# Which engine issues the first weight strips: three of four W1 strips move from SyncE to ScalarE

## The chip, the cores and the metric

The kernel runs on one core of a Trainium2 chip. The metric is the device time of one execution in microseconds (us). Before the change it is 163.12 us, the median of 3 runs (163.06 to 163.18).

## What is computed

x is 2048 rows of 512 bf16 numbers. Two branches and a gate are computed from it and mixed:

```python
qkv = x @ wqkv                    # 32 heads of 16
# a: each position attends to the 8 positions s, s-2, ..., s-14 of its head, then @ wo
h = layernorm(x, axis=-1)         # over the 512 columns, no weights
u = gelu(einsum("bsd,sf->bdf", h, w1) + b1)    # w1 is 2048 x 1792: it mixes the rows
b = transpose(einsum("bdf,fs->bds", u, w2) + b2)
g = sigmoid((x * gate_w).sum(-1, keepdims=True))
out = g * a + (1 - g) * b
```

## The kernel before

x is cut into 16 tiles X[:, t, :] of 128 rows (128 KB each). The first four of them are treated apart, and everything that this change concerns is in how they start.

**The lead.** For tiles 0 to 3, VectorE (DVE) takes the row statistics (`stat`, line 622; `aggr`, line 626), ScalarE (ACT) makes 1/sqrt(var) of them as Exp(-0.5 Ln(var)) (`rstd`, lines 629 and 630), and DVE writes the normalized tile LX (`apply`, line 633). TensorE (PE) then multiplies each with the first 512 columns of the same 128 rows of W1, a "strip" LW[:, t, :] of 128 KB, four matmuls to a tile (`f_lead`, line 617). PE also transposes the four x tiles (`f_tx`, line 585), the biases b1 and b2 (`f_tb`, lines 601 and 602) and spreads the gate's weights over the partitions by a matmul with ones ("gwbc", line 642). PE's order is written out by hand by a chain of order edges: five warm-up matmuls, tx0, tx1, the bias transposes, tx2, gwbc, lead0, tx3, lead1, lead2, lead3. ACT copies the transposed tiles from PSUM (`ext`), DVE the last one.

**After the lead.** PE computes the projections k, q, v (line 712, 192 matmuls) from the transposed x and WQKV; the first of them, "pjk", takes the first half of Wk ("wk01") alone. ACT copies them out. Then come W1 for all 16 tiles (line 608), W2 (line 937) and the output product with wo (line 946). DVE meanwhile multiplies q by shifted k, and the products are summed over a head's columns by 16 small matmuls for each half of the rows (line 803, "sum0" and "sum1"), which stand between the W1 matmuls in PE's order. Statistics of x tiles 4 to 15 (line 775) and the gate's sums (line 756) are DVE's too; those of tile 4 stand ahead of its first q-k product.

**What sets the order.** A small planner in the kernel (`_Sched`) simulates all operations with a duration for each and writes one fixed program for each engine. An operation waits for its producers by semaphores. Loads go through `load` (line 494; the DMA itself is at line 500, a transposing one at line 499). Those on SyncE's queue ("sp") are chained in the order in which the code names them: x0, x1, x2, strip 0, x3, strips 1, 2, 3, wk01, wk23, wq, x4 (tiles 4 and 5), then the transposing load xt1, x6, xt2, x8, xt3, x12, wv, W1 and so on. ACT issues three small loads in front of its work: b1, b2 and the gate's weights gw, which wait for POOL's zeroing of their tile (line 478). Its first table load stands behind these, because `emit_engine` puts a table load in front of the first activation that needs one:

```python
        def emit_engine(eng_name, e):
            table = None
            for op in sch.order[eng_name]:
                if eng_name == "act" and not op.is_dma:
                    want = TABLE.get(op.name, table or LOGEXP)
                    if want != table:
                        e.preload_act_table_set(want)
                        table = want
```

Of the kernel before, what the change touches and what calls it, by code (L numbers as in the profile page):

```python
# [13 lines left out]
D = 512  # L14
# [16 lines left out]
GL = 4  # L31
# [259 lines left out]
class _Mem:  # L291
# [17 lines left out]
    def view(self, name, dtype, dims, extra=0, p0=0, np_=128):  # L309
        base = self.arena[:].bitcast(dtype)  # L310
        pst = base.ap[0][0]
        esz = mybir.dt.size(dtype)
        o = self.off[name]
        assert o % esz == 0
        return bass.AP(base.tensor, p0 * pst + o // esz + extra, [[pst, np_]] + [list(d) for d in dims])


def bass_gated_mix__sliding_local_dilated__mixer_token_mlp__prompt_kernel(nc, A_x, A_wqkv, A_wo, B_x, B_w1, B_b1, B_w2, B_b2, gate_w, out, dbg=None):
    with contextlib.ExitStack() as es:
# [37 lines left out]
        def psub(ap_, p0, np_, offs, dims):  # L357
            pst = ap_.ap[0][0]
            return bass.AP(ap_.tensor, ap_.offset + p0 * pst + offs, [[pst, np_]] + [list(d) for d in dims])
# [9 lines left out]
        w1v = B_w1.rearrange("(st p) f -> p st f", p=128)  # L369
# [21 lines left out]
        LW = view("LOG", BF16, [(128 * GL, NLEAD), (1, 128 * GL)])  # L391
# [23 lines left out]
        GW1 = psub(GWZ, 0, 1, 0, [(1, D)])  # L415
# [10 lines left out]
        B1R = view("ROWS", BF16, [(1, 128)], np_=NFT)  # L426
        B2R = view("ROWS", BF16, [(1, 128)], extra=128, np_=NST)
# [30 lines left out]
        def col(v_, i):  # L458
            return bass.AP(v_.tensor, v_.offset + i, [list(v_.ap[0]), [1, 1]])
# [31 lines left out]

        last_ld = [None]

        def load(name, dst, src, nbytes, writes, transpose=False, queue="sp", issue=0.5, order=True, deps=(), reads=()):
            ds = sch.dsem(name)

            def fn(e):
                if transpose:
                    return e.dma_start_transpose(dst, src)
                return e.dma_start(dst, src)  # L500
            op = sch.dma(queue, fn, nbytes, ds, issue=issue, reads=reads, writes=writes, deps=deps,
                         after=([last_ld[0]] if order and last_ld[0] is not None else []), name=name)
            if order:
                last_ld[0] = op
            return op

        def ld_x(t0, n):
            load("x%d" % t0, X[:, t0:t0 + n, :], xv[:, t0:t0 + n, :], n * 128 * D * 2, ["x%d" % t for t in range(t0, t0 + n)])

        def ld_w(name, tn, d0, d1, res):  # L510
            load(name, WQKV[:, d0:d1, tn * D:(tn + 1) * D], wqkv_v[:, d0:d1, tn * D:(tn + 1) * D], (d1 - d0) * 128 * D * 2, [res])

        def ld_xt(sb):
            load("xT%d" % sb, XT[:, :, sb * 512:(sb + 1) * 512], x2d[sb * 512:(sb + 1) * 512, :], int(1.4 * 512 * D * 2), ["xt%d" % sb],
                 transpose=True)
# [1 line left out]
        def ld_wq(name, d0, d1, res):  # L517
            load(name, WQKV[:, d0:d1, 0:D], wqkv_v[:, d0:d1, 0:D], (d1 - d0) * 128 * D * 2, [res], queue="act", order=False)

        def ld_strip(t, n):  # L520
            load("s%d" % t, LW[:, t:t + n, :], w1v[:, t:t + n, 0:128 * GL], n * 32768 * GL, ["lw%d" % t_ for t_ in range(t, t + n)])

        ld_x(0, 1)
        ld_x(1, 1)
        ld_x(2, 1)
        ld_strip(0, 1)
        ld_x(3, 1)
        ld_strip(1, 1)
        ld_strip(2, 1)
        ld_strip(3, 1)  # L530
        ld_w("wk01", 1, 0, 2, "wk")
        ld_w("wk23", 1, 2, 4, "wk2")
        load("gw", GW1, bass.AP(gate_w.tensor, gate_w.offset, [[D, 1], [1, D]]), 1024, ["gwr"], issue=0.4, queue="act", order=False)
        load("b1", B1R, B_b1.rearrange("(t p) -> t p", p=128), 4096, ["b1r"], issue=0.4, queue="act", order=False)
        load("b2", B2R, B_b2.rearrange("(t p) -> t p", p=128), 4096, ["b2r"], issue=0.4, queue="act", order=False)
        ld_w("wq", 0, 0, 4, "wq")
        ld_x(4, 2)
        ld_xt(1)
# [53 lines left out]
        def ext(t, eng, after):  # L592
            bank, o = TXB[t]
            src = sub(psb(bank), o, [(128, 4), (1, 128)])
            dst = sub(XT, t * 128, [(S, 4), (1, 128)])
            if eng == "dve":
                return A("dve", lambda e: e.tensor_copy(out=dst, in_=src), 0.42, reads=["b%d" % bank], writes=["xt0_%d" % t], after=after, name="ext%d" % t, prio=-30)
            return A("act", act(dst, src, AF.Copy), 0.6, reads=["b%d" % bank], writes=["xt0_%d" % t], after=after, name="ext%d" % t, prio=-30)
# [69 lines left out]
        e3 = ext(3, "dve", [ag])  # L668
        l3 = apply(3, [e3])
        e3 = l3  # L670
# [61 lines left out]
        for dl in range(4):  # L732
# [3 lines left out]
          reads=["k%d_1" % dl for dl in range(4)], writes=["khalo"], name="khalo")  # L736
# [18 lines left out]
        for t in range(NST):  # L755
            A("dve", (lambda t_: lambda e: e.tensor_tensor_reduce(out=JUNK[:, t_ % 4, :], in0=X[:, t_, :], in1=GWB, scale=1.0, scalar=0.0, op0=ALU.mult, op1=ALU.add,  # L756
                                                                  accum_out=col(Z, t_)))(t), 0.61, reads=["x%d" % t, "gwb", "s4"], writes=["z%d" % t, "jk%d" % (t % 4)], after=[e3],
              name="z%d" % t, prio=-4)
        A("pool", lambda e: e.memset(ZN, 0.0), 0.15, writes=["zn"], name="zn0")
        A("dve", lambda e: e.tensor_scalar(out=ZN[:, 0:NST], in0=Z, scalar1=ZMAX, scalar2=-1.0, op0=ALU.min, op1=ALU.mult), 0.12,  # L760
          reads=["z%d" % t for t in range(NST)], writes=["zn"], name="zneg", prio=-30)
# [11 lines left out]

        for t in range(NLEAD, NST):
            A("dve", (lambda t_: lambda e: e.bn_stats(out=ST6[:, t_, :], in_=X[:, t_, :]))(t), 0.6,  # L775
              reads=["x%d" % t], writes=["st%d" % t], after=[e3], name="st%d" % t, prio=-4, delay=1.0 if t == 4 else 0.0)
        STS = ["st%d" % t for t in range(NLEAD, NST)]
        A("dve", tt(MS, ST_m0, ST_m1, ALU.add), 0.12, reads=STS, writes=["ms"], name="ln_ms", prio=-20)
        A("dve", tt(MD, ST_m0, ST_m1, ALU.subtract), 0.12, reads=STS, writes=["md"], name="ln_md", prio=-20)
# [4 lines left out]
          reads=["md"], writes=["vv"], name="ln_var", prio=-20)  # L784
# [3 lines left out]
          reads=["ms", "rstd"], writes=["nmr"], name="ln_nmr", prio=-20)  # L788
        for t in range(NLEAD, NST):
            if t >= NST - LNACT:  # L790
                A("act", act(X[:, t, :], X[:, t, :], AF.Identity, scale=col(RSTD2, t), bias=col(NMR, t)), 0.7, after=[ev2[0][t - NST - 1]], reads=["rstd", "nmr"], writes=["x%d" % t],
                  name="ln%d" % t)
            else:
                A("dve", (lambda t_: lambda e: e.tensor_scalar(out=X[:, t_, :], in0=X[:, t_, :], scalar1=col(MS, t_), scalar2=col(RSTD2, t_),
                                                               op0=ALU.subtract, op1=ALU.mult))(t), 0.33,
                  reads=["rstd", "ms", "st%d" % t], writes=["x%d" % t], name="ln%d" % t, prio=-4)
# [14 lines left out]
        for h in range(2):  # L811
# [43 lines left out]
            if h == 0:  # L855
                A("dve", tt(psub(LOG[0], 0, 32, 0, [(UT_, NW), (1, PAD)]), psub(LOG[0], 0, 32, 0, [(UT_, NW), (1, PAD)]), MASK, ALU.add), 0.2,
                  reads=["mask"], writes=["log0"], name="msk")
# [16 lines left out]
            for c in range(4):  # L874
                for dhi in range(4):
                    src = psub(ATT[h], 32 * c, 32, 0, [(1, NW * UT_)])
                    pst = AVW[h].ap[0][0]
                    dst = bass.AP(AVW[h].tensor, AVW[h].offset + dhi * pst + c * NW * UT_, [[4 * pst, 32], [1, NW * UT_]])
                    ds = sch.dsem("av%d_%d_%d" % (h, c, dhi))
                    prev = sch.dma("pool", (lambda d_, s_: lambda e: e.dma_start(d_, s_))(dst, src), 131072, ds, issue=1.0,  # L880
                                   reads=["att%d" % h], writes=["avw%d_%d_%d" % (h, c, dhi)] + al, after=[prev] if prev else [],
                                   name="av%d_%d_%d" % (h, c, dhi))
# [10 lines left out]
        for u in range(8):  # L893
# [5 lines left out]
              reads=["avw%d_%d_%d" % (h, c, dhi) for dhi in range(4)] + vr + ["vpad"], writes=PR[b], name="avm%d" % u)  # L899
# [15 lines left out]
        for ft in range(NFT):  # L915
            bank = ft if ft < GL else bank_()
            s0 = NLEAD if ft < GL else 0
            for a_, b_ in ((s0, 8), (8, NST)):
# [3 lines left out]
              reads=["b%d" % bank, "b1c"], writes=["ut%d" % ft] + (["wq", "wk", "wk2", "wv"] if ft == 0 else []), name="gel%d" % ft)  # L922
# [69 lines left out]
        for hf, (c0, c1) in enumerate(CH):  # L992
# [3 lines left out]
            if hf == 0:  # L996
                A("act", act(OUTS[:, NOUT, c0:c1], ps[:, bank, 0:n_], AF.Identity, scale=col(OMG, L), bias=col(C2, L)), 0.4,
                  reads=["b%d" % bank, "omg", "c2"], writes=["outl%d" % hf], name="ev%d_%d" % (L, c0))
# [5 lines left out]
        LOGEXP = "natural_log_exp_and_others"  # L1004
# [16 lines left out]

        def emit_engine(eng_name, e):
            table = None
            for op in sch.order[eng_name]:
                if eng_name == "act" and not op.is_dma:
                    want = TABLE.get(op.name, table or LOGEXP)
# [3 lines that stand above are left out]
                for d in op.waits:  # L1030
                    if d.is_dma:
                        e.wait_ge(d.dsem.handle, 16 * d.seq)
                    else:
                        e.wait_ge(esem[d.eng], d.seq)
                r = op.fn(e)
                if isinstance(r, list):
                    r = r[-1]
                if op.is_dma:
                    r.then_inc(op.dsem.handle, 16)
                elif op.sig:  # L1040
                    r.then_inc(esem[eng_name], 1)
            if eng_name == "sp":
                for d in ds_out + ds_last:
                    e.wait_ge(d.handle, 16 * d.count)

        emit_engine("sp", nc.sync)
        emit_engine("act", nc.scalar)
        emit_engine("pool", nc.gpsimd)
        emit_engine("dve", nc.vector)
        emit_engine("pe", nc.tensor)  # L1050
# [28 lines left out]
```

## Time and profile before

| | us |
|---|---|
| median of 3 runs | 163.12 (163.06 to 163.18) |
| profiled execution, its own time | 163.36 |
| span in the profile, first to last instruction | 162.1 |
| PE busy | 158.8 (98%) |
| DVE busy | 150.9 (93%) |
| ACT busy | 77.7 (48%) |
| POOL busy | 27.2 (17%) |

TensorE's granted clock is 1.0 throughout. The profile comes from one execution, which lies 0.24 us above the median; 1.26 us of its time lie outside the span.

How to read the views used below. The *chain of waits* follows the end back to the start: at each step to what released the instruction. Its rows are start, length, engine and line. In the *timeline* a row is start, length, engine, line, operation, tiles, count; in brackets stands how long the engine had been idle and what ended that. SPq and ACTq are DMA issues by SyncE and ScalarE, so a row of them is the issue, not the transfer. The *list of DMA issues* in a stretch gives, for the issues that fall in it, the time from issue to landing.

### The profile page before, as it was taken

How to read it: one execution, taken by the hardware profiler on the slowest of the kernel's cores; microseconds unless marked ns; L12 is line 12 of the kernel's file. 1: busy time of each engine (PE TensorE's matmuls, PEld its weight loads, DVE VectorE, ACT ScalarE, POOL GpSimd, SP SyncE). 2: the span in 40 equal slices, each digit the busy share in tenths (PEclk: the TensorE clock that was granted, in tenths of full speed). 3: DMA queues.
4: the chain of work that ended last, by engine and by line, in shares of the span. 5: the costliest groups of instructions: out<-in, count | busy, mean ns of one | idle time of the engine just before them, and what ended most of it. 6: DMA issues, size and time to landing. Idle time of an engine off the chain costs nothing.

```text
span 162.1 us, 2008 instructions
## 1 busy us (share of the span) xinstructions
PE 158.8 (98%) x778; PEld 75.7 (47%) x778; DVE 150.9 (93%) x143; ACT 77.7 (48%) x103; POOL 27.2 (17%) x63
## 2 busy tenths in 40 slices
PE   7999999999999999999999999999999999999994
PEld 3445555555554444444444444444444444444652
DVE  2968999999999999999999999999999999999963
ACT  3817765679999471699511344420111111111153
POOL 4000003000000002020595030007590003020000
DMA  4799989999952998999299999999999921959604
GB/s 132 224 258 209 243 194 328 257 213 212 287 174 82 298 294 193 240 266 216 55 311 363 350 299 306 212 297 289 345 220 204 194 92 50 200 131 194 142 32 162
DMA packets 45287, 35.54 MB, mean 219 GB/s; under 512 B 8029, under 2 KB 42078, under 8 KB 45278
## 3 DMA queue, kind: packets, MB, share of 16 engines
q1 hardware_dynamic: 41376, 22.74, 53.5%
q0 software_dynamic: 3696, 12.59, 35.6%
q8 instruction: 6, 0.10, 0.3%
q10 hardware_dynamic: 206, 0.08, 0.2%
q14 instruction: 3, 0.02, 0.0%
HBM read 19.15 MB, written 2.11 MB: 131 GB/s over the span
## 4 chain that ended last, share of the span: by engine, by line
PE 95%; DMA 2%; SPq 1%; DVE 0%; issue 0%
PE ps L937 30%; PE ps L608 28%; PE ps L712 26%; PE ps L946 9%; DMA arena<-in_B_w_dram 2%; PE ps L617 2%; SPq L500 1%; PE ps L803 1%; DVE arena L955 0%
## 5 line engine op out<-in xcount | busy, mean ns | idle before, releaser
L468 DVE TENSOR_TENSOR arena<-arena 128x4096 bf16<-128x4096 bf16 (+6 forms) x71 | 125.6, 1806 | 1.3
L937 PE MATMUL ps<-arena 128*128 128x512 bf16 (+2 forms) x238 | 50.2, 366 | 0.0
L471 ACT ACTIVATE arena<-ps,arena 128x512 bf16<-128x512 f32 (+1 forms) x29 | 20.9, 728 | 54.3 <-PE ps L946 40.1
L608 PE MATMUL ps<-arena 128*128 128x512 bf16 x208 | 45.4, 379 | 0.0
L712 PE MATMUL ps<-arena 128*128 128x512 bf16 x192 | 41.6, 379 | 0.0
L471 ACT ACTIVATE arena<-ps 128x512 bf16<-128x512 f32 (+3 forms) x38 | 31.7, 843 | 14.4 <-PE ps L712 11.1
L937 PEld LDWEIGHTS ps<-arena 128*128 128x128 bf16 x238 | 23.3, 98 | 25.4
L608 PEld LDWEIGHTS ps<-arena 128*128 128x128 bf16 x208 | 20.2, 98 | 24.9 <-issue 0.8
L712 PEld LDWEIGHTS ps<-arena 128*128 128x128 bf16 x192 | 21.7, 113 | 19.8 <-issue 0.3
L880 POOL DMA_DIRECT2D arena<-arena x32 | 17.1, 664 | 23.1 <-DVE arena L468 14.0
L471 ACT ACTIVATE arena<-arena 128x512 bf16<-128x512 bf16 (+6 forms) x27 | 15.2, 564 | 11.5 <-DVE arena L468 10.4
L946 PE MATMUL ps<-arena 128*128 128x512 bf16 (+2 forms) x68 | 15.6, 366 | 0.0
L831 POOL DMA_DIRECT2D arena<-arena x3 | 3.8, 1270 | 63.4 <-DVE arena L468 63.4
L1028 ACT ACT_TABLE_LOAD x9 | 11.5, 1283 | 2.3 <-POOL arena L479 2.2
L756 DVE CUSTOM_DVE_ANT_0 arena<-arena 128x512 bf16<-128x512 bf16 x16 | 10.1, 683 | 0.0
L901 POOL DMA_DIRECT2D arena<-arena x4 | 4.9, 1226 | 31.1 <-DVE arena L468 31.1
L946 PEld LDWEIGHTS ps<-arena 128*128 128x128 bf16 x68 | 6.6, 98 | 7.2
L775 DVE BATCH_NORM_STATS2 arena<-arena 128x6 f32<-128x512 bf16 x12 | 7.4, 680 | 2.3 <-DMA arena<-in_A_x_dram 2.3
L622 DVE BATCH_NORM_STATS2 arena<-arena 128x6 f32<-128x512 bf16 x4 | 2.7, 678 | 3.0 <-DMA arena<-in_A_x_dram 2.9
L617 PE MATMUL ps<-arena 128*128 128x512 bf16 x16 | 3.8, 378 | 0.2
L955 DVE TENSOR_SCALAR arena<-ps,arena 128x512 bf16<-128x512 f32 (+1 forms) x2 | 1.3, 659 | 2.7 <-PE ps L946 2.6
L567 PE MATMUL ps<-const-bfloat16-1.0 128*128 128x512 bf16 x5 | 2.3, 625 | 0.8 <-PEq L1064 0.8
(39 smaller groups left out, 18.7 us busy)
## 6 DMA issues: line engine op xcount, KB each, us to landing
arena<-in_B_w_dram SPq DMA_DIRECT2D x8, 896.0 KB, 13.5
arena<-arena POOLq DMA_DIRECT2D x6, 1024.0 KB, 9.8
arena<-in_B_w_dram SPq DMA_DIRECT2D x5, 1024.0 KB, 9.5
arena<-arena POOLq DMA_DIRECT2D x32, 128.0 KB, 7.5
arena<-arena POOLq DMA_DIRECT2D x1, 2048.0 KB, 17.9
out_dram<-arena SPq DMA_DIRECT2D x15, 128.0 KB, 1.8
arena<-in_B_w_dram SPq DMA_DIRECT2D x2, 768.0 KB, 13.4
arena<-in_A_wqkv_dram SPq DMA_DIRECT2D x2, 512.0 KB, 5.7
```

What stands on the lines that cost most here:

```text
L468: return lambda e: e.tensor_tensor(out=o_, in0=a_, in1=b_, op=op_)
L471: return lambda e: e.activation(out=o_, in_=i_, func=f_, **kw)
L608: ins = e.matmul(ps[:, bank, :], lhsT=W1S[W1AT[ft // 2]][:, st, 128 * (ft % 2):128 * (ft % 2) + 128], rhs=(LX if st < NLEAD else X)[:, st, :],
L617: ins = e.matmul(ps[:, ft, :], lhsT=LW[:, t, 128 * ft:128 * ft + 128], rhs=LX[:, t, :], start=(t == 0), stop=False)
L712: ins = e.matmul(ps[:, bank, :], lhsT=sub(WQKV, dt * 3 * D + tn * D + dl, [(4, 128)]), rhs=XT[:, dt, sb * 512:(sb + 1) * 512], start=(dt = ...
L756: A("dve", (lambda t_: lambda e: e.tensor_tensor_reduce(out=JUNK[:, t_ % 4, :], in0=X[:, t_, :], in1=GWB, scale=1.0, scalar=0.0, op0=ALU.m ...
L775: A("dve", (lambda t_: lambda e: e.bn_stats(out=ST6[:, t_, :], in_=X[:, t_, :]))(t), 0.6, reads=["x%d" % t], writes=["st%d" % t], after=[e ...
L880: prev = sch.dma("pool", (lambda d_, s_: lambda e: e.dma_start(d_, s_))(dst, src), 131072, ds, issue=1.0, reads=["att%d" % h], writes=["av ...
L901: sch.dma("pool", (lambda d_, s_: lambda e: e.dma_start(d_, s_, accum_op=ALU.add, max_dma_last_dim=4096))(sub(PB[b], 0, [(2048, 2), (1, 20 ...
L937: ins = e.matmul(ps[:, bank, 0:c1 - c0], lhsT=W2S[i // 2][:, ft, 128 * (i % 2):128 * (i % 2) + 128], rhs=UT[:, ft, c0:c1], start=(ft == 0) ...
L946: ins = e.matmul(ps[:, bank, 0:c1 - c0], lhsT=OT[:, i // 2, dl, 128 * (i % 2):128 * (i % 2) + 128], rhs=WO[:, dl, c0:c1], start=False, sto ...
L1028: e.preload_act_table_set(want)
```

## The change

- ACT's program begins with the table load, ahead of all its DMA issues.
- ACT then issues, in this order by order edges: b1, b2, strip 0, gw, strip 1, strip 2.
- SyncE issues x0, x1, x2, x3, strip 3, wk01, wk23, and then as before.
- In the planner's model, statistics and gate sums of tiles 6 and 7 get a delay of 1.0 each. It acts on the order alone. In the two programs the order of every engine's instructions is the same but for the DMA issues named here and the place of the first table load; so are the waits.

```diff
-        def ld_strip(t, n):
-            load("s%d" % t, LW[:, t:t + n, :], w1v[:, t:t + n, 0:128 * GL], n * 32768 * GL, ["lw%d" % t_ for t_ in range(t, t + n)])
+        def ld_strip(t, queue="sp", after=()):
+            return load("s%d" % t, LW[:, t, :], w1v[:, t, 0:128 * GL], 32768 * GL, ["lw%d" % t], queue=queue, order=queue == "sp", after=after)
 
         ld_x(0, 1)
         ld_x(1, 1)
         ld_x(2, 1)
-        ld_strip(0, 1)
         ld_x(3, 1)
-        ld_strip(1, 1)
-        ld_strip(2, 1)
-        ld_strip(3, 1)
+        ld_strip(3)
         ld_w("wk01", 1, 0, 2, "wk")
         ld_w("wk23", 1, 2, 4, "wk2")
-        load("gw", GW1, bass.AP(gate_w.tensor, gate_w.offset, [[D, 1], [1, D]]), 1024, ["gwr"], issue=0.4, queue="act", order=False)
-        load("b1", B1R, B_b1.rearrange("(t p) -> t p", p=128), 4096, ["b1r"], issue=0.4, queue="act", order=False)
-        load("b2", B2R, B_b2.rearrange("(t p) -> t p", p=128), 4096, ["b2r"], issue=0.4, queue="act", order=False)
+        prv = [load("b1", B1R, B_b1.rearrange("(t p) -> t p", p=128), 4096, ["b1r"], issue=0.5, queue="act", order=False)]
+        prv = [load("b2", B2R, B_b2.rearrange("(t p) -> t p", p=128), 4096, ["b2r"], issue=0.5, queue="act", order=False, after=prv)]
+        prv = [ld_strip(0, queue="act", after=prv)]
+        prv = [load("gw", GW1, bass.AP(gate_w.tensor, gate_w.offset, [[D, 1], [1, D]]), 1024, ["gwr"], issue=0.3, queue="act", order=False, after=prv)]
+        prv = [ld_strip(1, queue="act", after=prv)]
+        prv = [ld_strip(2, queue="act", after=prv)]
...
-              name="z%d" % t, prio=-4)
+              name="z%d" % t, prio=-4, delay=1.0 if t in (6, 7) else 0.0)
...
-              reads=["x%d" % t], writes=["st%d" % t], after=[e3], name="st%d" % t, prio=-4, delay=1.0 if t == 4 else 0.0)
+              reads=["x%d" % t], writes=["st%d" % t], after=[e3], name="st%d" % t, prio=-4, delay=1.0 if t in (4, 6, 7) else 0.0)
...
         def emit_engine(eng_name, e):
             table = None
+            if eng_name == "act":
+                e.preload_act_table_set(LOGEXP)
+                table = LOGEXP
```

More of the change, by code (lines that the diff above doesn't have):

```diff
@@ L492, in bass_gated_mix__sliding_local_dilated__mixer_token_mlp__prompt_kernel, with load @@
         last_ld = [None]
-        def load(name, dst, src, nbytes, writes, transpose=False, queue="sp", issue=0.5, order=True, deps=(), reads=()):
+        def load(name, dst, src, nbytes, writes, transpose=False, queue="sp", issue=0.5, order=True, deps=(), reads=(), after=()):
             ds = sch.dsem(name)
@@ L501, in load @@
             op = sch.dma(queue, fn, nbytes, ds, issue=issue, reads=reads, writes=writes, deps=deps,
-                         after=([last_ld[0]] if order and last_ld[0] is not None else []), name=name)
+                         after=list(after) + ([last_ld[0]] if order and last_ld[0] is not None else []), name=name)
             if order:
```

## The prediction, made before the changed kernel ran

> **What bounds the kernel now.** I read the page's busy shares first (PE 98%, DVE 93%), then the chain of waits in order of time, which says where PE's 98% begins to count.
>
> ```profile
> 2.74 0.43 SPq L500
> ...
> 3.21 3.15 DMA arena<-in_B_w_dram
> 6.37 0.14 issue
> 6.50 2.75 PE ps L617 x12
> 9.25 41.44 PE ps L712 x192
> ```
>
> The chain is SyncE's queue of issues up to the one at 3.21 us, which is strip 1; its landing at 6.37; then lead1 at 6.50 and PE to the end, without a hole. So the end moves only with the start of that unbroken stretch: the 12 matmuls of leads 1 to 3 and, behind them, the projections at 9.09. The timeline of the first 13 us shows who else is near that path:
>
> ```profile
> 0.81 1.02 ACTq L500 DMA_DIRECT2D arena<-in_B_b_dram  x2
> ...
> 1.86 0.28 ACTq L500 DMA_DIRECT2D arena<-in_gate_w_dram  x1
> ...
> 2.17 1.28 ACT L1028 ACT_TABLE_LOAD   x1 [2.17 <-POOL arena L479]
> ...
> 3.87 0.44 ACT L471 ACTIVATE arena<-arena 128x1 f32<-128x1 f32 x2 [0.41 <-DVE arena L626]
> ...
> 5.95 0.23 PEld L585 LDWEIGHTS ps<-arena 128*128 128x128 bf16 x4 [0.58 <-DMA arena<-in_A_x_dram]
> ...
> 7.54 0.41 DVE L633 TENSOR_SCALAR arena<-arena 128x512 bf16<-128x512 bf16 x1 [0.19 <-ACT arena L471]
> ...
> 12.83 0.69 DVE L775 BATCH_NORM_STATS2 arena<-arena 128x6 f32<-128x512 bf16 x1 [2.27 <-DMA arena<-in_A_x_dram]
> ```
>
> ACT's first Ln comes at 3.87; its table load ended at 3.45 and so costs nothing now. PE waits 0.58 us for x3 ahead of tx3. DVE works through the lead with small gaps until the last normalized tile (7.54 to 7.95), and later stands 2.27 us until x4 has landed. One more row matters, from the timeline of PE's weight loads around 56 us:
>
> ```profile
> 56.66 0.55 PEld L803 LDWEIGHTS ps<-arena 128*32 128x32 bf16 x16 [0.42 <-DVE arena L468]
> ```
>
> DVE's product sum runs 52.12 to 56.55 and releases sum0 at 56.66. DVE has hardly a gap between x4's landing and there, so the chain from x4 is about level with PE's own. PE can be some 0.1 us later before it alone decides; it can be earlier at the end only if x4 is earlier too.
>
> **The change, part by part.**
>
> *SyncE.* Three strips leave its queue: 0.51 + 0.44 + 0.44 us and gaps (issue rows 2.19, and 1.39 for three from 3.21). x3 is issued at about 2.19 instead of 2.74, strip 3 at 2.65 instead of 4.17, wk01 at 3.15 instead of 4.65, wq and x4 1.5 us earlier, and xt1 at 5.2 instead of 6.70.
>
> *ACT's issues.* Before: 1.02 for the two bias loads, 0.28 for gw. Added: three strips at 0.46 each with a gap of 0.04. From 0.81, if the table load only stands ahead and lets the issues pass: b1 and b2 to 1.83, strip 0 from 1.86 (before 2.19), gw from 2.36 (before 1.86), strip 1 from 2.67 (before 3.21), strip 2 from 3.17 to 3.65 (issue before 3.68). That is 0.2 ahead of the first Ln, which waits behind them in ACT's program and whose input, DVE's aggregate, comes at 3.83. Behind the Ln stands the whole lead: Exp, `apply`, lead0, and all later rows of ACT.
>
> Does an issue wait until the table load has run? No row shows an ACT issue behind busy ACT work. Bounds: 0, and the row's 1.28 us. I take 0: in the nearest rows the load starts 0.03 after gw's issue ended, as if one small dispatcher handed out both, and a dispatcher need not wait for the engine. [...]
>
> Do issues from two engines slow each other? b1, issued at the same moment as x0, took 0.66 and b2 0.33 (the longest and shortest issue of that row); SyncE's issues beside them were no longer than later ones. Bounds 0 and 0.33 for each strip; I take 0, the row of SyncE's issues.
>
> *Transfers.* By the list of DMA issues the landings are: x2 at 4.1, strip 0 at 4.7, x3 2.74 + 3.2 = 5.9, strip 1 3.21 + 3.2 = 6.4, wk01 4.65 + 4.3 = 8.95, wq 12.0, x4 6.15 + 6.7 = 12.85. Between 2.2 and 9.2 us the DMA engines are 70 to 100% busy at 172 to 270 GB/s. The time from issue to landing grows from 2.1 (x0) to 6.7: from x3 on the wait is for bandwidth, not for the issue. The bytes ahead of wk01 are the same in both kernels, so an earlier issue brings only what the engines idled, up to about 0.25 of 3 us: 0 to 0.7 us for strip 1, x3, wk01 and x4. I take 0.4 for strip 1, 0.3 for the others.
>
> *The lead, again.* lx0 still at 4.75, so lead0 not before 4.84; strip 0 (1.86 + 2.5 = 4.4, or 4.9 with half the bandwidth) and gwbc (gw 2.36 + 2.1 = 4.5, one copy behind strip 0 on its queue) put it at 4.85 to 5.0. A lead takes 0.87 (four matmuls at 0.217): tx3 at 5.75 with x3 there or nearly, lead1 at 6.05 to 6.2 instead of 6.50, lead2 at 7.0. Then the next thing is late: lead3 needs lx3. On DVE only the 0.07 us before tile 3's statistics (5.93) goes away, so lx3 ends at 7.87 at best, lead3 starts at 7.95, and the projections at 8.82 instead of 9.09. **PE gains at most 0.27 us**, with wk01 landing at 8.65 to 8.95 more like 0.15 to 0.25. x4's 0.3 lets DVE follow by as much. The table load's new place saves nothing, since its end at 3.45 was not waited for.
>
> Sum: profiled execution 163.36 (162.1 in the span, 1.26 around it) less 0.17 is 163.19; the median lies 0.24 lower: **162.95**.
>
> **The rivals.**
>
> *ACT is still issuing when its first Ln is due* (ends slower). Place: the Ln at 3.87. The chain over lx3 has 0.29 us of room (7.95 against lead3's start at 9.09 - 0.87 = 8.22); from an issue end of 4.2 on, every tenth is a tenth at the end. If the table load holds the issues, they end at 3.65 + 1.28 = 4.93: Ln 1.06 later, less 0.29 and less 0.07 at sum0: +0.7, 163.8. If each strip's issue takes 0.33 longer: 4.64, +0.4, 163.5. For: no row shows either absent. Against: the dispatch rows above. Chance 0.2.
>
> *The strips take bandwidth from x2 and x3.* On SyncE's queue x2 was ahead of all strips; on two queues strip 0 runs beside it. If both get half of 250 GB/s, x2 (128 KB) lands 0.5 later, at 4.6 to 4.9, and x3 by 6.3; tx2 stands ahead of gwbc and lead0, so lead0 starts at 5.3 to 5.5, and lead1 at 6.5 to 6.7: between 0 and +0.2 at the end, and +0.4 if tile 2's statistics (4.76) wait too and lx3 slips with them. [...] 163.2 to 163.5; chance 0.17, of which 0.05 above +0.33.
>
> *Nothing arrives earlier.* The transfers are bound by bytes, x4 lands at 12.8 as before, and sum0 waits for DVE whatever PE gained: 163.05 to 163.15. For: the issue-to-landing times; SyncE's transposing issue xt1 (6.70 to 12.70) ends just before x4's landing, and the same pairing holds for xt2 (16.01) with x6 (16.15), as if these wait for the queue to run dry. Chance 0.2.
>
> *More than the bound*, from something that this trace doesn't show (below 162.79): 0.08.
>
> **How the numbers follow.** Forecast, a gain of 0.05 to 0.3: 0.35, the likeliest. About 0.33 us is 0.2%, which is what a measurement of this kernel can tell from no change; the forecast lies within it because lx3 caps it. Faster by over 0.2%: 0.1 (the 0.08 and a little of the forecast's edge). Slower: 0.05 from the bandwidth rival and most of the first, 0.23 together. Same: 0.67. The range goes from 162.7 to 163.9, to take in the held table load.
>
> **What would show it.** Right: ACT's table load at 0.81 with ACTq rows inside it and the last of these ended by 3.7; Ln at 3.87; lead1 at 6.0 to 6.2; lx3 at 7.9; projections at 8.8 to 8.95; x4's wait on DVE ending before 12.83. ACTq rows that start only at 2.1 and an Ln near 4.9 show the first rival; tx2 waiting for x2 shows the second; sum0's weights waiting for DVE at 56.6 with a hole in PE shows the third. I'm wrong altogether if something past 13 us moves the end.

## The result: slower by 0.5%

| | before | changed |
|---|---|---|
| median of 16 runs, us | 163.51 (162.99 to 164.31) | 164.20 (163.57 to 165.85) |
| ratio, 95% interval | | 1.0048 (1.003 to 1.0066) |
| profiled execution / its span | 163.36 / 162.1 | 164.28 / 163.0 |
| lead0, lead1, lead2 start (lead2 before: 6.50 + 0.87) | 4.84, 6.50, 7.37 | 5.54, 6.63, 8.28 |
| projections start | 9.09 | 10.00 |

The change costs 0.69 us at the median; the forecast was a gain of 0.17. (The runs beside the changed kernel also put the kernel before at 163.51 instead of 163.12, so 0.39 of the distance between 162.95 and 164.20 is the base.) The changed kernel also scatters more: two of its 16 runs lie at 165.6 and 165.9, and the kernel before has none above 164.3. Medians in this document are over all executions, while the ratios leave out those more than 1.5% above the fastest of their kernel (none here, and below two of the twelve of hold_wk and one of s13_act).

The chain of waits of the changed kernel, in order of time:

```profile
1.73 3.21 DMA arena<-in_A_x_dram
4.93 0.05 issue
4.98 0.40 PE ps L585 x4
...
8.30 1.87 PE ps L617 x8
10.16 41.44 PE ps L712 x192
```

The unbroken stretch is as long as before (41.44 us of projections, and all that follows); it starts 0.91 later, which is the whole difference of the two spans. The chain now runs over the landing of x2 at 4.93 us (before: 4.1), which holds tx2. The timeline of the same kernel shows the rest:

```profile
0.80 1.28 ACT L1025 ACT_TABLE_LOAD   x1 [0.80 <-PEq L1067]
...
0.84 0.99 ACTq L500 DMA_DIRECT2D arena<-in_B_b_dram  x2
...
2.67 0.86 ACTq L500 DMA_DIRECT2D arena<-in_B_w_dram  x2
...
3.80 0.44 ACT L471 ACTIVATE arena<-arena 128x1 f32<-128x1 f32 x2 [1.72 <-DVE arena L626]
...
4.98 0.40 PE L585 MATMUL ps<-arena 128*128 128x128 bf16 x4 [0.80 <-DMA arena<-in_A_x_dram]
...
6.63 1.03 PE L617 MATMUL ps<-arena 128*128 128x512 bf16 x4
...
8.28 1.89 PE L617 MATMUL ps<-arena 128*128 128x512 bf16 x8 [0.62 <-DVE arena L674]
...
11.48 0.69 DVE L775 BATCH_NORM_STATS2 arena<-arena 128x6 f32<-128x512 bf16 x1 [0.75 <-DMA arena<-in_A_x_dram]
```

ACT issues its first load at 0.84, inside the table load, and its first Ln comes at 3.80: the issues did not wait for the load. lead1 is only 0.13 later than before. TensorE runs from tx2 to lead1 without a gap, so this 0.13 comes from x2; strip 1 landed at 2.67 + 3.8, about 0.2 ahead of lead1. Lead1's four matmuls, 0.217 apart, end their turn at 7.50; then TensorE stands for about 0.8 us until lead2 at 8.28. The row puts this down to DVE's line 674, but lead2 reads neither of DVE's copies of the biases: it reads lx2, ready at 7.11, and strip 2. So the part of the chain that is left out above, which runs through DVE to these copies, is not what made lead2 late. The list of DMA issues, for strip 2's issue at 3.08 us (ACTq) beside strip 3's at 2.67 (SPq), gives size and time to landing:

```profile
arena<-in_B_w_dram SPq DMA_DIRECT2D x1, 128.0 KB, 4.0
arena<-in_B_w_dram ACTq DMA_DIRECT2D x1, 128.0 KB, 5.1
```

Strip 2 lands at 3.08 + 5.1 = 8.2. In the kernel before, its issue at 3.70 has this row:

```profile
arena<-in_B_w_dram SPq DMA_DIRECT2D x1, 128.0 KB, 3.0
```

There it was issued 0.6 later and landed at 3.70 + 3.0 = 6.7. So in this execution 0.13 of the 0.91 comes in with lead1, by x2, and 0.78 is strip 2.

### The profile page after: what moved, and what is told of

The parts are those of the page before. It is cut to its first block, busy times and chain, and to the rows that moved or that the text cites. A ratio compares the mean times of both kernels' runs of the same rounds, so it can differ in the third digit from the quotient of the medians.

```text
span 163.0 us, 2008 instructions
## 1 busy us (share of the span) xinstructions
PE 158.6 (97%) x778; PEld 75.9 (47%) x778; DVE 151.1 (93%) x143; ACT 77.7 (48%) x103; POOL 27.2 (17%) x63
## 4 chain that ended last, share of the span: by engine, by line
PE 94%; DMA 2%; DVE 1%; ACT 1%; SPq 1%; issue 0%
PE ps L937 30%; PE ps L608 28%; PE ps L712 25%; PE ps L946 8%; DMA arena<-in_A_x_dram 2%; PE ps L803 1%; PE ps L617 1%; ACT arena L471 1%; DVE arena L633 1%; SPq L500 1%; DVE arena L955 0%; PE ps L585 0%; PE ps L642 0%; DVE arena L626 0%; DVE arena L674 0%
## 6 DMA issues: line engine op xcount, KB each, us to landing
arena<-in_B_w_dram SPq DMA_DIRECT2D x8, 896.0 KB, 12.9
```

## The experiments

The theories: **A**, Wk's loads, which SyncE now issues at 3.15, take bandwidth from the strips on ScalarE's queue, which are needed sooner. **B**, the first profile caught a chance stall. **C** came up with the first run: TensorE runs at half speed through the leads in some executions. (The expectations say that it falls to half speed. In every trace here its first matmuls of 128x512 follow each other by about 0.43 us, called half speed below, and the 0.217 of full speed comes once and stays through the leads; what differs is when it comes.) Each kernel was timed beside the kernel before on the same chip. "Above 165" counts executions over 165.0 us.

| kernel | median, us | before beside it | ratio, 95% interval | above 165 | profiled execution, us | its projections start |
|---|---|---|---|---|---|---|
| after_again | 165.12 | 163.67 | 1.0098 (1.0066 to 1.0131) | 4 of 6 | 165.30 | 11.02 |
| swap23 | 164.88 | 163.67 | 1.0091 (1.0057 to 1.0126) | 3 of 6 | 163.60 | 9.31 |
| s23_sync | 163.92 | 163.67 | 1.0050 (1.0017 to 1.0082) | 3 of 12 | 163.84 | 9.52 |
| table_first | 163.48 | 163.67 | 1.0004 (0.9987 to 1.0021) | 0 of 12 | 163.45 | 9.17 |
| fill | 163.93 | 163.44 | 1.0027 (1.0015 to 1.0040) | 0 of 12 | 163.88 | 9.56 |
| swap23_fill | 164.14 | 163.44 | 1.0036 (1.0023 to 1.0048) | 0 of 12 | 163.69 | 9.37 |
| before_nowarm | 164.48 | 163.44 | 1.0060 (1.0039 to 1.0080) | 3 of 10 | 165.11 | 10.84 |
| s13_act | 163.67 | 163.44 | 1.0019 (0.9997 to 1.0042) | 2 of 12 | 163.83 | 9.57 |
| hold_wk | 163.50 | 163.57 | 1.0010 (0.9983 to 1.0038) | 3 of 12 | 163.22 | 8.83 |
| hold_wk_swap | 163.55 | 163.57 | 1.0019 (0.9992 to 1.0045) | 2 of 12 | 163.51 | 9.24 |
| x3_first | 163.38 | 163.57 | 0.9994 (0.9978 to 1.0011) | 0 of 12 | 163.42 | 9.14 |
| before_fill | 163.51 | 163.57 | 1.0003 (0.9986 to 1.0020) | 0 of 12 | 164.00 | 9.43 |
| hold_wk_fill1 | 163.64 | 163.50 | 1.0003 (0.9989 to 1.0018) | 0 of 12 | 163.97 | 9.69 |
| hold_wk_fill2 | 163.71 | 163.50 | 1.0013 (0.9998 to 1.0029) | 0 of 12 | 163.28 | 8.98 |

The kernel before had no execution above 165 in any of these groups (highest 164.08).

In fourteen of the sixteen profiles of this document the execution took 154.3 us (154.26 to 154.32) from the start of the projections, whatever the edit; hold_wk took 154.39 and before_fill 154.57. So it is the start of the projections that decides the time. A profile tells about its one execution, which can lie far from the median: swap23's took 163.60 beside a median of 164.88.

### The changed kernel again

> The changed kernel, unaltered, profiled once more. Theory A (strip 2): the last strip on ScalarE's queue shares the DMA engines with the Wk loads that SyncE now issues early, so it lands 1.4 us later than before (8.18 against 6.77 us) and lead2 waits for it. A expects lead2 again about 8.0 to 8.6 us, the projections about 9.8 to 10.3, and the time 0.5 to 1.0 us over the kernel before. Theory B (a chance stall): one slow stretch of some DMA engines at 2.5 to 3 us in that one execution made x2, strip 2 and the rest late. B expects lead2 at about 7.4 here, the projections near 9.2, and the surplus of the time from something past the lead.

Strip 2 landed at 3.07 + 5.2 = 8.3 again, so B is out for it. But lead2 (9.29) and the projections came 1.0 later than in the first profile, outside A's ranges too, and 4 of 6 executions lay above 165. Strip 2 had been there for 1.0 when lead2 began: in this execution it held nothing up. TensorE's timeline of this run:

```profile
4.86 0.61 PE L585 MATMUL ps<-arena 128*128 128x128 bf16 x4 [0.63 <-DMA arena<-in_A_x_dram]
5.26 0.63 PE L642 MATMUL ps<-arena,const-bfloat16-1.0 128*128 128x512 bf16 x1
5.69 1.91 PE L617 MATMUL ps<-arena 128*128 128x512 bf16 x4
7.39 0.63 PE L585 MATMUL ps<-arena 128*128 128x128 bf16 x4
7.82 3.36 PE L617 MATMUL ps<-arena 128*128 128x512 bf16 x12
11.02 0.38 PE L712 MATMUL ps<-arena 128*128 128x512 bf16 x1
```

Four lead matmuls take 1.91 where the first profile has 1.03, and the one at L642 0.63 where it had 0.39. The rows of line 617, minimum, median and maximum in ns, say the same; first the changed kernel's first profile, then this one:

```profile
L617 PE MATMUL ps<-arena x16: 376/379/379, 5.5 to 9.8; 128*128 128x512 bf16 x16
```

```profile
L617 PE MATMUL ps<-arena x16: 379/380/634, 5.7 to 10.8; 128*128 128x512 bf16 x16
```

The page of the kernel before has both speeds too, in its leads and in its five warm-up matmuls (count, busy us, mean ns, idle before):

```profile
L617 PE MATMUL ps<-arena 128*128 128x512 bf16 x16 | 3.8, 378 | 0.2
...
L567 PE MATMUL ps<-const-bfloat16-1.0 128*128 128x512 bf16 x5 | 2.3, 625 | 0.8 <-PEq L1064 0.8
```

In this run the lead matmuls are the same as in the first profile, their starts 0.43 us apart up to 9.1 us and 0.217 from there. The granted clock reads 1.000 in this run too: that column does not show it. This trace holds no clock record, nor do those of the first two profiles, so the 1.0 says nothing of their first microseconds. Nine of the other traces hold one, in their trace files; it first reads full speed at 3.7 to 6.6 us, and in each the spacing of TensorE's instructions shortens there (hold_wk_swap: 5.83, with lead0's matmuls at 5.29, 5.72, 6.00 and 6.21). What sets that moment no view here shows; before_nowarm, below, moves it.

### Strips 2 and 3 exchanged; both on SyncE

```diff
-        ld_strip(3)
+        ld_strip(2)
...
-        prv = [ld_strip(2, queue="act", after=prv)]
+        prv = [ld_strip(3, queue="act", after=prv)]
```

> The changed kernel with strips 2 and 3 exchanged: SyncE issues strip 2 (behind x3), ScalarE issues strip 3 last. A: strip 2 lands about 6.7, strip 3 about 8.2; lead2 follows lead1 without a wait at 7.5 and lead3 at 8.4, since strip 3 is needed 0.87 us later than strip 2; projections at 9.25 instead of 10.0; the time 0.7 us below the changed kernel, within 0.2 us of the kernel before. B: no difference from the changed kernel beyond chance.

Strip 2 lands at 2.66 + 4.1 = 6.8, strip 3 at 3.07 + 4.7 = 7.8. All three leads run without a hole, in TensorE's timeline of swap23:

```profile
6.73 2.75 PE L617 MATMUL ps<-arena 128*128 128x512 bf16 x12 [0.22 <-DMA arena<-in_B_w_dram]
9.31 0.38 PE L712 MATMUL ps<-arena 128*128 128x512 bf16 x1
```

The step that A names is confirmed in this execution (9.31, expected 9.25), the time is not: half of the executions lie above 165.

```diff
         ld_x(3, 1)
-        ld_strip(3)
+        ld_strip(2)
+        ld_strip(3)
...
-        prv = [ld_strip(2, queue="act", after=prv)]
```

> The changed kernel with strips 2 and 3 both on SyncE, behind x3 and ahead of Wk; ScalarE issues strips 0 and 1 only. A: strip 2 lands about 6.6, strip 3 about 7.3, Wk's first half about 8.7; projections at 9.2 to 9.3, set by lead0, which still starts at 5.5 because of x2 and gw; time within 0.2 us of the kernel before. B: as the changed kernel.

Here strip 2 is early enough, but strip 1, on ScalarE's queue, landed at 2.65 + 4.1 = 6.8 and held lead1 to 6.94: 9.52 instead of 9.2 to 9.3. lead0 came at 4.83, not at 5.5, since x2 had landed at 4.2. Again 3 of 12 above 165, and the time is 0.5% above the kernel before, not within 0.2 us of it.

### The table load alone

The kernel before, with the change's lines in `emit_engine` and nothing else.

```diff
             table = None
+            if eng_name == "act":
+                e.preload_act_table_set(LOGEXP)
+                table = LOGEXP
```

> The kernel before with one part of the change alone: the table load ahead of ScalarE's three small issues. Theory of the prediction: the issues run beside the load (b1 at 0.84, first Ln at 3.8 to 3.9), nothing waits, time as the kernel before within 0.1 us. Rival (the load holds the issues): b1 at 2.1, the bias transposes and gwbc wait, lead0 later than 5.0, time 0.3 us or more above.

As the theory had it: b1 at 0.84, the first Ln at 3.80, a ratio of 1.0004. The table load's place is neutral.

### Dummy matmuls in the hole

```diff
         PE(f_tb, 0.2, ["b1r", "b2r", "ident"], ["b7"], "t_b12")
+        PE(f_warm(2, 0), 0.1, [], ["b0"], "fill")
```

> The changed kernel with two more dummy matmuls on TensorE between the bias transposes and tx2, where it stands idle for x2 (0.97 us in the first profile, 0.80 in the second). Theory C: this hole, and what it does to TensorE's speed, costs more than the wait itself: in the second profile the first 8 lead matmuls follow each other by 0.43 us (634 ns each in the profile) and in the first by 0.217 (379 ns), so in some executions the leads run at half speed and the projections start near 11.0 instead of 10.0. C expects no execution above 165.0 us, all lead matmuls at 379 ns, and a median near 164.1. Theory A alone (strip 2 late, nothing else): the same spread as the changed kernel, 163.6 to 166.

None of 12 above 165, median 163.93: as C had it. Strip 2 was late here too: lead2 at 7.84, where lead1 at 6.59 and 0.87 would give 7.46.

The same two dummies and the exchange of strips 2 and 3:

> Both remedies at once: strips 2 and 3 exchanged, and the two dummy matmuls. If A and C are the two parts of the loss, the projections start at 9.2 to 9.4 in every execution and the time is within 0.3 us of the kernel before, without a group above 165. If only A holds, the exchange with its group above 165 (three of six) comes back. If only C holds, the projections start near 10.

No group above 165 and projections at 9.37, but 0.7 us (0.36%) over the kernel before instead of within 0.3. The two dummies ran at 0.40 and 0.43 from start to start in its profile and put tx2 to 5.0 and lead0 to 5.7; x2 had landed at 4.1 and lead0's strip at 4.5. So this remedy costs part of what it saves. The profiled execution is one of the fastest (163.69); what the median, 0.45 above it, consists of is not shown.

### The kernel before with one warm-up matmul instead of five

```diff
-        PE(f_warm(5, 0), 2.1, [], ["b0"], "warm0")
+        PE(f_warm(1, 0), 2.1, [], ["b0"], "warm0")
```

> The kernel before with one warm-up matmul instead of five, all else as it was. C: TensorE has done too little by 4.8 us, lead0 and some of the others run at 0.43 a matmul; lead1 to lead3 are then 12 x 0.217 = up to 2.6 us longer, and the time is 0.8 to 2.6 us above. A rival without the speed of TensorE: nothing changes, since the warm-up matmuls end at 3.0, before x0 is used.

Line 617 in this run:

```profile
L617 PE MATMUL ps<-arena x16: 379/561/635, 5.2 to 10.6; 128*128 128x512 bf16 x16
```

Half speed until about 9.2, projections at 10.84, 0.6% slower. Nothing of the DMAs was changed: TensorE stood idle for 1.64 us from 1.43, where the other four warm-up matmuls had been, and in this execution the leads were slow. The profiled execution is the slowest of the ten (165.11); the others go down to 163.61 without a break, so there is no separate group above 165 here. The size is as expected, at the lower end. This profile and after_again's, the only ones of executions above 165, are the only two in which full speed came after 9 us.

### Strip 0 back on SyncE

Lines of the changed kernel; gw's line also moves, to behind b2's.

```diff
         ld_x(2, 1)
+        ld_strip(0)
         ld_x(3, 1)
-        ld_strip(3)
+        ld_strip(2)
...
-        prv = [ld_strip(0, queue="act", after=prv)]
         prv = [ld_strip(1, queue="act", after=prv)]
-        prv = [ld_strip(2, queue="act", after=prv)]
+        prv = [ld_strip(3, queue="act", after=prv)]
```

> The changed kernel with strip 0 back on SyncE behind x2, strip 2 too (behind x3), and gw ahead of the strips on ScalarE, which issues strips 1 and 3 only. Theory D: x2 and gw are late because strip 0 shares the DMA engines with x2 and stands ahead of gw. D expects x2 at 4.1 (4.93 in the changed kernel), gw at 4.2 or before, tx2 at 4.2 to 4.4, lead0 at 4.85 to 5.1, lead1 at 6.2 to 6.5, no hole in which TensorE loses its speed, and a time within 0.2 us of the kernel before or up to 0.2 below. If D is wrong, x2 stays near 4.9 and so does the group above 165.

x2 landed at 4.1, and gwbc followed tx2 without a gap at 4.52, so gw was in time, as D had it; but strip 0, now beside strip 1, landed at 5.25 and lead0 waited to 5.39, and lead1 came at 6.98. The hole had moved, not gone: 2 of 12 above 165. D is right on x2 in this profile, and wrong on the leads. That x2 must be late with strip 0 beside it does not hold: it landed at 4.1 to 4.2 in swap23, s23_sync and fill as well, with the same loads ahead of it, and at 4.8 to 4.9 in the changed kernel's two profiles.

### Wk held until x3 has landed

```diff
-        ld_x(3, 1)
+        x3 = ld_x(3, 1)
...
-        ld_w("wk01", 1, 0, 2, "wk")
+        ld_w("wk01", 1, 0, 2, "wk", deps=[x3])
```

> The changed kernel with one wait more: SyncE issues Wk's first half only when x3 has landed (about 5.3 us instead of 3.15), so the strips on ScalarE's queue share the DMA engines with x3 and strip 3 alone. A (strips 1 and 2 are late because Wk, which nobody needs before 9 us, takes half of the bandwidth): strip 1 lands at 5.7 to 6.2 (6.43 in the changed kernel), strip 2 at 6.2 to 6.9 (8.14), lead2 follows lead1 without a wait, and the projections start at 8.9 to 9.4, set by strip 1 or by Wk's landing at about 8.6 to 9. Rival E (ScalarE's queue is served worse whatever else runs): strip 2 again near 8, projections near 10. The hole ahead of tx2 is still there, so some executions above 165 are expected by C.

Strip 2's landing, then TensorE's timeline of this run:

```profile
arena<-in_B_w_dram ACTq DMA_DIRECT2D x1, 128.0 KB, 3.4
```

```profile
5.15 1.03 PE L617 MATMUL ps<-arena 128*128 128x512 bf16 x4
6.02 0.39 PE L585 MATMUL ps<-arena 128*128 128x128 bf16 x4
6.24 2.75 PE L617 MATMUL ps<-arena 128*128 128x512 bf16 x12
8.83 0.59 PE L712 MATMUL ps<-arena 128*128 128x512 bf16 x2
```

Strip 2 lands at 3.07 + 3.4 = 6.5 instead of 8.2 with the same issue time on the same queue; only Wk, and what is queued behind Wk, was taken from beside it. The two versions with dummies and Wk held, below, give 6.7 and 6.6, fill without the hold 7.7. A is shown, the rival E falls: with Wk held, strip 2 took 3.4 on ScalarE's queue and strip 3, issued at 2.66, took 3.5 on SyncE's. The projections start at 8.83, 0.26 before the kernel before, and the span is 161.9. Some 0.1 of the 0.26 is lost again later, at sum0's weights:

```profile
56.51 0.55 PEld L803 LDWEIGHTS ps<-arena 128*32 128x32 bf16 x16 [0.45 <-DVE arena L468]
```

This is the sign that the prediction named for its third rival: x4, queued behind Wk, lands at 6.71 + 6.2 = 12.9 again, and PE, now earlier, waits for DVE. The nine executions that are not in the group above 165 have a median of 163.33 beside 163.57. With the three that are, it is no gain: over all twelve the mean is 163.95 beside 163.54, and the ratio of 1.001 leaves out two of the three.

The same edit with strips 2 and 3 exchanged and gw's line ahead of strip 0's:

> The same wait ahead of Wk, strips 2 and 3 exchanged, and gw issued ahead of strip 0. A: every lead finds its strip; lead0 at 4.9 to 5.4, lead1 at 6.0 to 6.4, projections at 8.85 to 9.2, so the time between 0.2 us below and 0.1 above the kernel before, but for executions in which x2 comes late and TensorE falls to half speed. E: projections at 9.3 or later.

The leads found their strips, but tx2, gwbc and lead0's first matmul ran at half speed, so lead1 came at 6.65: projections at 9.24, just outside A's range and short of E's, as in C (tx2 took 0.61 and gwbc 0.63, where hold_wk has 0.46 and 0.38).

### Order on one queue, and a dummy in the kernel before

In x3_first SyncE issues x3 ahead of strip 0, all else as in the kernel before.

```diff
-        ld_strip(0, 1)
         ld_x(3, 1)
+        ld_strip(0, 1)
```

> The kernel before with one exchange on SyncE's queue: x3 ahead of strip 0, all strips still on SyncE. The kernel before is then bound by bytes: strip 1 stays sixth on the queue and lands at 6.2 to 6.5; lead1 starts at 6.4 to 6.6 and the time is within 0.15 us of the kernel before, although x3 is 0.5 us earlier, and lead0 0.3 to 0.6 later. The step of the prediction that let an earlier x3 help expects lead1 at 6.05 to 6.2 and 0.2 us less.

Strip 1 landed at 5.9, earlier than expected, and yet lead1 started at 6.55: lead0 now waited for strip 0 until 5.47, and tx3 and lead1 stood behind it. x3 at 4.4 brought nothing. The time is that of the kernel before.

```diff
         PE(f_tb, 0.2, ["b1r", "b2r", "ident"], ["b7"], "t_b12")
+        PE(f_warm(1, 0), 0.1, [], ["b0"], "fill")
```

> The kernel before with one dummy matmul more, behind the bias transposes. C, in its wider form (the scatter of the kernel before, 163.0 to 164.0, is also the moment at which TensorE reaches full speed): the executions at 163.5 to 164.0 become fewer, the median falls by 0.1 to 0.3. If the scatter has another source (landings): no change, or up to 0.2 more, since the dummy puts tx2 0.4 later.

No difference. The scatter of the kernel before is not shown to be TensorE's speed.

### Both parts removed

hold_wk with the dummy line of fill, for one dummy (`f_warm(1, 0)`) and for two (`f_warm(2, 0)`).

> The changed kernel with Wk held until x3 has landed, and one dummy matmul behind the bias transposes. If the loss has two parts only (A: Wk takes bandwidth from the strips; C: TensorE falls to half speed in the hole ahead of tx2), then the projections start at 8.8 to 9.1 and fewer executions than 3 of 12 (held Wk without a dummy) lie above 165: median 163.2 to 163.5 beside about 163.5 for the kernel before. If a third part remains, projections start later than 9.2 at full speed.

> The same with two dummy matmuls. C: no execution above 165. They put tx2 at 4.6 to 5.0 and lead0 at 5.0 to 5.7, which lead1 feels only where it would start before 6.6: projections at 8.9 to 9.4, time within 0.2 us of the kernel before.

None of 24 executions above 165, and both intervals of the ratio take in 1 (up to 1.0018 and 1.0029, beside 1.0048 for the change): with Wk held and the hole filled, no loss can be told. The one dummy's profile still had lead0 at half speed (0.43 from 5.44) and projections at 9.69, and its median of 163.64 is above the expected 163.2 to 163.5; the two dummies' profile had projections at 8.98. No version tried beats the kernel before.

## Why the prediction was wrong

The forecast was 0.17 us less, and the sign was wrong.

- **The step that failed is the one on transfers**: "an earlier issue brings only what the engines idled ... I take 0.4 for strip 1, 0.3 for the others". The issues came as early as forecast, and for the other loads that it names the step was not too high: x3 landed 0.4 earlier (2.20 + 3.3 = 5.5), Wk's first half 0.3 (3.15 + 5.5 = 8.65), x4 1.3 (DVE's wait for it ended at 11.48 instead of 12.83). Strip 1, issued 0.55 earlier, landed no earlier (about 6.45 against 6.37). Strip 2, for which the sum has no term at all, was issued 0.6 earlier and landed 1.5 later (8.2 against 6.7): that is 0.78 of the 0.91. The gain went to Wk and x4, which did not set the end here, and was paid by the strips. The step counted the bytes ahead of Wk and took the order among them as kept. On SyncE's single queue the strips had stood ahead of Wk; on two queues they ran beside it. hold_wk shows this: with Wk held, strip 2 lands at 6.5 and the projections start at 8.83.
- **The bandwidth rival had the right mechanism and stopped too early.** It let strip 0 take from x2 and x3, and gave 0.05 to more than +0.33. Its own numbers came true in this profile (x2 at 4.93 for 4.6 to 4.9, lead0 at 5.54 for 5.3 to 5.5, lead1 at 6.63 for 6.5 to 6.7), which is the 0.13; that strip 0 was the reason is not shown, since x2 landed at 4.1 to 4.2 in four other profiles with the same loads ahead of it (swap23, s23_sync, fill, swap23_fill). Strip 2 was never costed: "lead2 at 7.0. Then the next thing is late: lead3 needs lx3". lead2 came at 8.28, behind strip 2. Sharing between two queues was weighed for the transfers around strip 0 only; for the pair that counted, strip 2 and Wk, hold_wk shows it (strip 2 at 8.2 beside Wk, at 6.5 with Wk held).
- **TensorE's speed was not in the prediction.** The profile of before had the sign of it: on its page the five warm-up matmuls (line 567) have a mean of 625 ns and the same shape at line 617 has 378. So "TensorE's granted clock is 1.0 throughout" was no ground to leave it out. Holes near 5 us were treated as plain waits. In the seven groups of runs with strips on both queues and no dummies, 19 of 76 executions lay above 165; in the four with dummies, none of 48. In the first comparison it was 2 of 16, so it moves that median little (164.14 without the two). The 0.6 that is left fits the strips: without the executions above 165, hold_wk has 163.33. With two dummies the kernel has a ratio of 1.0027 without the hold (fill) and 1.0013 with it (hold_wk_fill2), which points the same way, but these intervals overlap. Of the executions above 165 two were profiled, both with the leads at half speed; for the others it is inferred from the dummies.
- **Right:** the issues passed the table load (0.84 inside 0.80 to 2.08; table_first 1.0004); strips took 0.38 to 0.44 each to issue on ScalarE, beside SyncE's, with no lengthening (0.43 to 0.51 on SyncE before); the first Ln is not delayed (3.80). The first rival fell. So did the third for the changed kernel: x4 came earlier, and sum0 did not wait for DVE. In hold_wk, where PE is earlier and x4 is not, it takes 0.1.
- **Right where the strips arrive, in part by luck:** the cap by lx3, "8.82 instead of 9.09", is what hold_wk measured (8.83), with lx3 ready at 7.87 as forecast. But there PE also runs without a gap from lead0 at 5.15 to the projections, so lead3 would have come at 7.97 without lx3's cap too. (The room that the first rival gives lx3 is 0.27 by its own figures, 8.22 less 7.95, and not 0.29.)

Left open: why x2 landed at 4.8 to 4.9 in two profiles of the changed kernel and at 4.1 to 4.6 in others with the same loads ahead of it, and in which executions of a kernel full speed comes late.

## What to carry to other kernels

In the profile of before the loads on SyncE's one queue landed in the order of their issue (x2 at 4.1, strip 0 at 4.7, x3 at 5.9, strips 1 to 3 at 6.4, 6.7 and 7.9, Wk's first half at 8.9). With strips on ScalarE's queue, Wk went out at 3.15 instead of 4.65 and ran beside strip 2, which landed at 8.2, and at 6.5 with Wk held. So list what moves up when loads go to a second queue, and hold back (by a wait on a landing) what is needed later; here that removed the loss and brought no gain. Issue time was 0.45 us a load here, and it was not what the strips waited for. Look at the matmul durations of the first microseconds as well: of two executions with strip 2 equally late, the one in which full speed came only at 9.1 us was 1 us longer.

## What the runs showed of the hardware

- ScalarE issued DMAs while a table load ran: in the changed kernel two issues (0.84 to 1.83) within the load (0.80 to 2.08).
- TensorE's matmul of 128x512 took 0.43 us start to start in the first microseconds and 0.217 later. Full speed came at 3.7 to 6.6 us in the executions whose trace has a clock record, at 9.1 to 9.2 in after_again and before_nowarm, where the profile's clock column reads 1.000 for want of a record.
- x4, the copy ahead of the transposing load xt1 on SyncE's queue, landed about when xt1's issue ended, in three runs: at 12.8 with the issue ending at 12.70 before, at 11.5 with 11.34 in the changed kernel, at 12.9 with 12.86 in hold_wk. So the transposing issue's length (6.00, 6.12 and 5.60) looks like a wait and not like a price of its own; what it waits for was not tried.
